# Two transformer layers on one core: another order for attention's product trees, a first q projection in four passes, wq rows ahead of the x tiles, other places for later loads

## The chip, the cores and the metric

The kernel runs on one core of a Trainium2 chip. The metric is the device time of one execution in microseconds (us). Each version was run several times; medians are quoted. A profile is one of the executions, recorded by the hardware profiler; its span is about 1.8 us shorter than the time of the same run (1616.3 against 1618.12 us).

Names: PE is TensorE (matmuls), PEld its weight loads, DVE VectorE, ACT ScalarE, SP the engine whose queue issues nearly all DMAs ("SPq" in the profile).

## The reference

```python
x = x + A(layernorm(x))      # attention, four times in all: A, B, A, B
x = x + B(layernorm(x))      # gated MLP
# A: qkv = x @ wqkv;  32 heads of 32;  each token attends to 8 tokens: itself and
#    those 2, 4, ... 14 back (dilation 2);  softmax;  @ wo
# B: (silu(x @ w1) * (x @ w3)) @ w2
```

x is 2048 tokens x 1024, F is 3584, everything in bf16.

## The kernel before

PE does the projections and the MLP. Attention itself has no matmuls: because each token sees only 8 others, DVE forms the products elementwise and adds them up in *trees*. Tokens are handled in chunks of 512 (c = 0 to 3), attention in halves of a chunk (256 tokens). In this program the order of the instructions on each engine is the order in which it emits them. A small clock model in the program (`now`, `pe()`, `dve()`) decides where DVE's attention steps are interleaved; it fixes an order, it does not wait for anything.

One tree multiplies and adds up 8 times; a product lives in one of two buffers (`scr`):

```python
scr = ctx.enter_context(tc.tile_pool(name="scr", bufs=2))
...
def tree(n, mul, dst):
    bufs = {}
    def first(i):                      # product, 128 x 2048
        bufs[i] = mul(i)
    def half(i, m):                    # add the upper half to the lower one
        b = bufs[i]
        if m > 1:
            nc.vector.tensor_tensor(b[:, 0:m, :], b[:, 0:m, :], b[:, m:2 * m, :], op=ALU.add)
        else:
            nc.vector.tensor_tensor(dst(i), b[:, 0, :], b[:, 1, :], op=ALU.add)
    yield 1.14, 0.0, lambda: first(0)
    for i in range(n):
        yield 0.605, 0.0, lambda: half(i, 4)
        if i:
            yield 0.21, 0.0, lambda: half(i - 1, 1)
        if i + 1 < n:
            yield 1.14, 0.0, lambda: first(i + 1)
        yield 0.34, 0.0, lambda: half(i, 2)
    yield 0.27, 0.0, lambda: half(n - 1, 1)
```

Each attention half runs two trees: one gives the scores, the other the output `oT`. PE then multiplies `oT` by wo in *output-projection tiles* of 128 tokens (16 matmuls named `po`). The first four of these (called tiles 1 to 4 below; 1 and 2 need the first half's oT, 3 and 4 the second's, that is the fourth tree) are placed among the projections of chunk 3.

At the start, wq (8 rows of 256 KB) and four token tiles of x come in while PE warms up; the first q projection is made tile by tile:

```python
load_tile(0, 0, 512, nc.sync); load_tile(0, 512, D, nc.scalar); load_tile(1, 0, D, nc.sync)
loads(0, 2)                    # wq rows 0, 1
load_tile(2, 0, D, nc.sync)
loads(2, 4)
load_tile(3, 0, D, nc.sync)
loads(4, 8)                    # ... then K's weights and x of chunk 1 (1 MB each)
...
warm(NWARM)                    # 13 matmuls on zeros
# (cut) tokens 0-127: kk outermost, as the wq rows arrive; tokens 128-255: block by block
tok = slice(2 * P, CH)         # tokens 256-511 in one pass
for i, acc in enumerate(accumulators(2, 2 * P)):
    for b in range(2):
        for kk in range(KT):
            product(acc[:, b, :], kk, 2 * i + b, tok, kk == 0, kk == KT - 1)
    nc.scalar.copy(hT[:, 2 * i:2 * i + 2, tok], acc[:])
    nc.sync.dma_start(q_rows[:, 2 * i:2 * i + 2, 0:CH], hT[:, 2 * i:2 * i + 2, :])
    then[i]()    # load_x(2), V's weights, V's weights, load_x(3)
```

Then comes K of chunk 0 (matmuls named `ps`), whose results go to DRAM by way of SP, four stores of two blocks each. The statistics of *all* chunks of x stand ahead of the first tree on DVE.

Of the kernel before, what the change touches and what calls it, by code (L numbers as in the profile page):

```python
# [15 lines left out]
def kernel(  # L16
# [13 lines left out]
    nc = tc.nc  # L30
# [17 lines left out]
    scale = float(Dh) ** -0.5  # L48
    EPS = 1e-5
    BOOST = 3000  # L50
    NWARM = 13
    fsplits = [(0, 16), (16, NF)] if NF > 16 else [(0, NF)]
    HTN = max(b - a for a, b in fsplits)

# [25 lines left out]


    MM, TABLE, DMA = 0.216, 1.3, 2.5
    now = dict(pe=22.0, dve=15.0, act=22.0, table=None)
    units = [(l, c) for l in range(2) for c in range(NCH)]
    norms, attention = [], []
    x_at = [12.5, 20.0, 25.0, 34.0]
    xnT_at, norm_left, qkv_at, oT_at, o_todo = {}, {}, {}, {}, {}

    def pe(n, ready=0.0):
# [137 lines left out]
        for part in parts:  # L227
            norms.append([part(key, c, r), None])

    def first_q(ws, loads, then):  # L230


        xnT = xnTs["Q", 0, 0] = xtp.tile([P, KT, CH], BF16, name="xnT")
        st = small.tile([P, TPC, 2, 6], FP32, name="st1", bufs=1)
        mv = small.tile([P, TPC, 2], FP32, name="mv1", bufs=1)
        sd = small.tile([P, TPC], FP32, name="sd1", bufs=1)
        rstd = small.tile([P, TPC], FP32, name="rstd1", bufs=1)
        q_rows = qkv_d[0][0][:].rearrange("i t s -> (i t) s").rearrange("(b p) s -> p b s", p=P)

        def load_tile(j, h0, h1, queue):  # L240
            queue.dma_start(x_sb[:, j, h0:h1], xin[:, j, h0:h1])  # L241

        load_tile(0, 0, 512, nc.sync)
        load_tile(0, 512, D, nc.scalar)
        load_tile(1, 0, D, nc.sync)
        loads(0, 2)
        load_tile(2, 0, D, nc.sync)
        loads(2, 4)
        load_tile(3, 0, D, nc.sync)
        loads(4, 8)  # L250
        preload = small.tile([P, 1], FP32, name="preload", bufs=1)
        nc.scalar.activation(preload[:], epst[:], ACTF.Sqrt)

        def stats(j, hh):
            nc.vector.bn_stats(st[:, j, hh, :], x_sb[:, j, hh * 512:(hh + 1) * 512])  # L255

        def deviation(j):
            nc.vector.bn_aggr(mv[:, j, :], st[:, j, :, :])
            nc.scalar.activation(sd[:, j:j + 1], mv[:, j, 1:2], ACTF.Sqrt, bias=epst[:])  # L259

        def apply(j, parts=1):
            nc.vector.reciprocal(rstd[:, j:j + 1], sd[:, j:j + 1])
            xn = xnp.tile([P, D], BF16, name="xn")
            for i in range(parts):
                d = slice(i * D // parts, (i + 1) * D // parts)
                nc.vector.tensor_scalar(xn[:, d], x_sb[:, j, d], mv[:, j, 0:1], rstd[:, j:j + 1],  # L266
                                        op0=ALU.subtract, op1=ALU.mult)
            return xn

        def transpose(xn):  # L270
            pTs = []
            for h in range(2):
                pT = psum.tile([P, KH, P], BF16, name="pT", tag="mm")
                for kk in range(KH):
                    nc.tensor.transpose(pT[:, kk, :], xn[:, (h * KH + kk) * P:(h * KH + kk + 1) * P], ident[:])  # L275
                pTs.append(pT)
            return pTs

        def evacuate(j, h, pTs, copy):
            copy(xnT[:, h * KH:(h + 1) * KH, j * P:(j + 1) * P], pTs[h][:])  # L280

        def product(out, kk, b, tok, start, stop):
            nc.tensor.matmul(out, lhsT=ws[kk // KH][:, kk % KH, b * P:(b + 1) * P], rhs=xnT[:, kk, tok],  # L283
                             start=start, stop=stop, skip_group_check=True)

        def accumulators(per, n):
            return [psum.tile([P, per, n], FP32, name="pq", tag="mm") for _ in range(KT // per)]

        warm(NWARM)
        stats(0, 0)  # L290
        stats(0, 1)
        deviation(0)
        stats(1, 0)
        xn = apply(0, 2)
        pTs = transpose(xn)
        evacuate(0, 0, pTs, nc.scalar.copy)
        stats(1, 1)
        evacuate(0, 1, pTs, nc.vector.tensor_copy)
        deviation(1)

        accs = accumulators(4, P)
        tok = slice(0, P)

        def step0(kk):
            for b in range(KT):
                product(accs[b // 4][:, b % 4, :], kk, b, tok, kk == 0 and b % 4 == 0, kk == KT - 1)

        for kk in range(6):
            step0(kk)
        stats(2, 0)  # L310
        xn = apply(1)
        pTs = transpose(xn)
        for h in range(2):
            evacuate(1, h, pTs, nc.scalar.copy)
        for kk in range(6, KT):
            step0(kk)
        stats(2, 1)
        deviation(2)
        for i in range(2):
            nc.scalar.copy(hT[:, 4 * i:4 * i + 4, tok], accs[i][:])  # L320

        accs = accumulators(4, P)
        tok = slice(P, 2 * P)

        def block1(b):
            for kk in range(KT):
                product(accs[b // 4][:, b % 4, :], kk, b, tok, kk == 0, kk == KT - 1)
            if b % 4 == 3:
                nc.scalar.copy(hT[:, b - 3:b + 1, tok], accs[b // 4][:])

        stats(3, 0)
        xn = apply(2)
        stats(3, 1)
        deviation(3)
        for b in range(3):
            block1(b)
        pTs = transpose(xn)
        for h in range(2):
            evacuate(2, h, pTs, nc.scalar.copy)
        xn = apply(3)  # L340
        for b in range(3, 5):
            block1(b)
        pTs = transpose(xn)
        evacuate(3, 0, pTs, nc.scalar.copy)
        evacuate(3, 1, pTs, nc.vector.tensor_copy)
        for b in range(5, KT):
            block1(b)

        tok = slice(2 * P, CH)
        for i, acc in enumerate(accumulators(2, 2 * P)):  # L350
            for b in range(2):
                for kk in range(KT):
                    product(acc[:, b, :], kk, 2 * i + b, tok, kk == 0, kk == KT - 1)
            nc.scalar.copy(hT[:, 2 * i:2 * i + 2, tok], acc[:])
            nc.sync.dma_start(q_rows[:, 2 * i:2 * i + 2, 0:CH], hT[:, 2 * i:2 * i + 2, :])
            then[i]()
        qkv_at[0, 0, 0] = now["act"] + DMA / 2

    def tree(n, mul, dst):

        bufs = {}

        def first(i):
            bufs[i] = mul(i)

        def half(i, m):
# [3 lines that stand above are left out]
            else:  # L370
                nc.vector.tensor_tensor(dst(i), b[:, 0, :], b[:, 1, :], op=ALU.add)  # L371

        yield 1.14, 0.0, lambda: first(0)
        for i in range(n):
            yield 0.605, 0.0, lambda: half(i, 4)
            if i:
                yield 0.21, 0.0, lambda: half(i - 1, 1)
            if i + 1 < n:
                yield 1.14, 0.0, lambda: first(i + 1)
            yield 0.34, 0.0, lambda: half(i, 2)  # L380
        yield 0.27, 0.0, lambda: half(n - 1, 1)

    qks, vs = {}, {}

# [296 lines left out]
    def load_wq(k0, k1):  # L681
        for kk in range(k0, k1):
            nc.sync.dma_start(w_tiles[kk // KH][:, kk % KH, :], wqkv_v[:, kk, 0:D])  # L683
        if k1 == KT:
            load_weight()
            load_weight()
            load_x(1)

    first_q(w_tiles[0:2], load_wq, (lambda: load_x(2), load_weight, load_weight, lambda: load_x(3)))
    xnT_at["Q", 0, 0], norm_left["Q", 0, 0] = now["pe"], 0  # L690
    queue_norm(("Q", 0, 1), 1, 0)
    queue_norm(("Q", 0, 1), 1, 1)
# [3 lines left out]
    for c in range(NCH):  # L696
        for which in range(3):
            if c == NCH - 1 and which == 0:
                o_queue += [(0, n) for n in range(TPC)]
            if c == NCH - 1 and which == 2:  # L700
                between(False, True)
            then = ()
            if c == 0 and which == 0:
                continue
            if c == 2 and which == 0:
                then = (None, None, lambda: nc.sync.dma_start(wo[:], wo_v))
            if c == 2 and which == 1:
                then = (load_weight, None, load_weight)
            q_part(0, c, which, w_tiles[2 * which:2 * which + 2], then)
            if c == NCH - 1:  # L710
                release(2)
            if which == 0 and 1 <= c < NCH - 1:
                for r in range(R):
                    queue_norm(("Q", 0, c + 1), c + 1, r, (norm_apply,))
# [44 lines left out]
```

## Time and profile before

| | before |
|---|---|
| median time (6 runs) | 1619.05 us (1618.66 to 1619.55) |
| span of the profiled run | 1616.3 us (the time of this run was 1618.12 us) |
| PE busy | 1610.7 us |
| DVE busy | 1176.6 us (73%) |
| first `ps` matmul | 24.64 us |
| first tree begins | 47.74 us |

The first lines of the page: span, and busy us, share of the span and instructions of each engine.

```profile
span 1616.3 us, 19263 instructions
...
PE 1610.7 (100%) x7609; PEld 805.3 (50%) x7609; DVE 1176.6 (73%) x1965; ACT 353.6 (22%) x547; POOL 1.9 (0%) x12
```

The chain of waits in order of time (start, us, what): followed back from the last instruction, it stays on PE from 16.48 us. The last line here is output-projection tile 3, in 3.45 us without a break. (The chain's times lie 0.16 to 0.17 us behind those of the timeline, below.)

```profile
16.48 8.33 PE pq L283 x88
24.80 113.96 PE ps L591 x528
...
159.49 3.45 PE po L552 x16
```

A 512-wide `ps` matmul takes 113.96 / 528 = 0.216 us. The Trainium skill, "TensorE: Matmul & The Clock Gate", section "Wait — 56ns, not 53.3ns?", gives N / 2.4 GHz plus about 2.5 ns for warm matmuls, 215.7 ns at N = 512; this trace agrees. So PE already runs there at the rate that the page calls warm, and what is left to gain is its waiting.

The timeline of the first 80 us (start us, duration us, engine, line, operation; in brackets the idle time before it and what ended it): the waits for wq rows, the first `ps`, the issue of x of chunk 3, the statistics of chunk 3, and the first trees.

```profile
8.92 0.45 PEld L283 LDWEIGHTS <-wqkv 128*128 128x128 bf16 x8 [0.24 <-DMA wqkv<-in_A_wqkv_dram]
...
10.24 0.45 PEld L283 LDWEIGHTS <-wqkv 128*128 128x128 bf16 x8 [0.87 <-DMA wqkv<-in_A_wqkv_dram]
...
24.64 55.63 PE L591 MATMUL ps<-xnT,wqkv 128*128 128x512 bf16 x257
...
25.86 0.98 SPq L677 DMA_DIRECT2D x_sb<-in_A_x_dram  x1
...
40.93 1.27 DVE L189 BATCH_NORM_STATS2 st<-x_sb 128x6 f32<-128x512 bf16 x2
...
47.74 1.21 DVE L424 TENSOR_TENSOR pr<-qT,kT 128x2048 bf16<-128x2048 bf16 x1
...
51.66 0.29 DVE L371 TENSOR_TENSOR psm<-pr 128x256 bf16<-128x256 bf16 x1
...
51.99 1.23 DVE L424 TENSOR_TENSOR pr<-qT,kT 128x2048 bf16<-128x2048 bf16 x1
...
54.38 1.23 DVE L424 TENSOR_TENSOR pr<-qT,kT 128x2048 bf16<-128x2048 bf16 x1
```

One step of a tree, product to product, takes 54.38 - 51.99 = 2.39 us; the product starts 0.33 us after the last small fold. x of chunk 3 (`x_sb`, L677) is issued at 25.86 us; its statistics run at 40.93 without a wait for a DMA.

Last, the wait of PE's weight loads for attention (us in total, times, longest), the one thing on PE that DVE delayed after the start:

```profile
PEld L552 <- DVE oT L371: 0.2, 1, 0.2
```

### The profile page before, as it was taken

The page shows a single profiled execution, that of the slowest core. Times are in us where ns is not written, and L with a number is a line of the kernel's source. Part 1 is how long each engine was busy: PE and PEld are TensorE (multiplying, and loading weights), DVE is VectorE, ACT ScalarE, POOL GpSimd, SP SyncE. Part 2 cuts the span into 40 slices and gives each one's busy share as a digit, 9 for nine tenths or more (in the row PEclk, how much of TensorE's full clock was granted, in tenths as well). Part 3 has the DMA queues.
Part 4 walks back from the last instruction along what each step waited for, and adds up shares of the span by engine and source line. Part 5 has one row for each costly group of instructions (what it writes and reads, how often), then busy time and mean ns, then how long its engine had stood idle before and what let it go on. Part 6 is the DMA issues. An engine that isn't in the chain of part 4 may idle for free.

```text
span 1616.3 us, 19263 instructions
## 1 busy us (share of the span) xinstructions
PE 1610.7 (100%) x7609; PEld 805.3 (50%) x7609; DVE 1176.6 (73%) x1965; ACT 353.6 (22%) x547; POOL 1.9 (0%) x12
## 2 busy tenths in 40 slices
PE   9999999999999999999999999999999999999999
PEld 6666544444445544455444554445544444444444
DVE  5999898989899899998998449983599832222212
ACT  4433311212112230222302123021230212011110
POOL 0000000000000000000000000000000000000000
PEclk9999999999999999999999999999999999999999
DMA  9565855466537773577553776528684266436440
GB/s 314 149 190 158 254 178 169 129 193 190 170 105 236 222 203 125 169 208 249 160 186 120 211 239 175 186 97 259 210 223 158 93 194 170 143 108 218 157 130 27
DMA packets 336427, 285.82 MB, mean 177 GB/s; under 512 B 69712, under 2 KB 318928, under 8 KB 336208
## 3 DMA queue, kind: packets, MB, share of 16 engines
q1 hardware_dynamic: 336192, 284.46, 58.0%
q8 instruction: 59, 0.97, 0.2%
q14 instruction: 32, 0.26, 0.0%
q10 hardware_dynamic: 144, 0.13, 0.0%
HBM read 239.47 MB, written 29.36 MB: 166 GB/s over the span
## 4 chain that ended last, share of the span: by engine, by line
PE 99%; DMA 0%; SPq 0%; DVE 0%; ACT 0%; issue 0%
PE acc L658 24%; PE pu L642 24%; PE pg L634 24%; PE ps L591 20%; PE po L552 7%; PE pq L283 1%; DMA wqkv<-in_A_wqkv_dram 0%; SPq L683 0%; SPq L241 0%; DVE xn L266 0%; ACT xnT L280 0%; PE pT L275 0%; DVE st L255 0%; ACT sd L259 0%; DVE x_sb L668 0%
## 5 line engine op out<-in xcount | busy, mean ns | idle before, releaser
L642 PE MATMUL pu<-xnT,w3t 128*128 128x512 bf16 x1792 | 423.4, 379 | 0.0
L634 PE MATMUL pg<-xnT,w1t 128*128 128x512 bf16 x1792 | 423.4, 379 | 0.0
L658 PE MATMUL acc<-w2t,hT 128*128 128x512 bf16 (+1 forms) x1804 | 389.7, 378 | 0.0
L591 PE MATMUL ps<-xnT,wqkv 128*128 128x512 bf16 x1472 | 319.2, 379 | 0.0
L638 ACT ACTIVATE sg<-pg 128x512 bf16<-128x512 f32 x224 | 133.6, 597 | 773.0 <-PE pg L634 719.4
L646 DVE TENSOR_TENSOR hT<-sg,pu 128x512 bf16<-128x512 bf16 x224 | 152.6, 681 | 186.8 <-PE pu L642 177.8
L658 PEld LDWEIGHTS <-hT 128*128 128x128 bf16 x1804 | 176.5, 98 | 210.5
L642 PEld LDWEIGHTS <-w3t 128*128 128x128 bf16 x1792 | 175.4, 98 | 211.4
L634 PEld LDWEIGHTS <-w1t 128*128 128x128 bf16 x1792 | 175.3, 98 | 211.4
L591 PEld LDWEIGHTS <-wqkv 128*128 128x128 bf16 x1472 | 211.1, 143 | 106.7
L424 DVE TENSOR_TENSOR pr<-qT,kT 128x2048 bf16<-128x2048 bf16 x128 | 156.2, 1221 | 87.2 <-DMA kT<-qkv_d 85.1
L668 DVE TENSOR_TENSOR x_sb<-x_sb,acc 128x512 bf16<-128x512 bf16 x129 | 87.3, 677 | 107.6 <-PE acc L658 107.4
L484 DVE TENSOR_TENSOR tm<-At,vT 128x2048 bf16<-128x2048 bf16 x128 | 156.1, 1220 | 2.4
L595 ACT CAST sgt<-ps 128x512 bf16<-128x512 f32 x184 | 106.7, 585 | 230.7 <-PE ps L591 211.9
L369 DVE TENSOR_TENSOR tm<-tm 128x1024 bf16<-128x1024 bf16 (+1 forms) x256 | 134.5, 550 | 0.4
L369 DVE TENSOR_TENSOR pr<-pr 128x1024 bf16<-128x1024 bf16 (+1 forms) x256 | 134.0, 551 | 0.5
L552 PE MATMUL po<-wo,oT 128*128 128x512 bf16 x512 | 115.7, 379 | 0.0
L552 PEld LDWEIGHTS <-oT 128*128 128x128 bf16 x512 | 50.1, 98 | 60.1 <-DVE oT L371 0.2
L189 DVE BATCH_NORM_STATS2 st<-x_sb 128x6 f32<-128x512 bf16 x120 | 75.9, 671 | 4.6 <-DMA x_sb<-in_A_x_dram 4.6
L557 DVE TENSOR_TENSOR x_sb<-x_sb,po 128x512 bf16<-128x512 bf16 x64 | 43.3, 684 | 19.2 <-PE po L552 18.9
L638 ACT ACT_TABLE_LOAD x31 | 39.8, 1283 | 51.2 <-PE pg L634 51.0
L446 DVE STREAM_TRANSPOSE psmT<-psm 128x2048 bf16<-128x2048 bf16 x16 | 36.9, 2306 | 0.2
(85 smaller groups left out, 402.3 us busy)
## 6 DMA issues: line engine op xcount, KB each, us to landing
w1t<-in_B_w_dram SPq DMA_DIRECT2D x56, 1024.0 KB, 5.5
w3t<-in_B_w_dram SPq DMA_DIRECT2D x56, 1024.0 KB, 8.0
w2t<-in_B_w_dram SPq DMA_DIRECT2D x48, 1024.0 KB, 5.4
wqkv<-in_A_wqkv_dram SPq DMA_DIRECT2D x28, 1024.0 KB, 6.8
qkv_d<-sgt SPq DMA_DIRECT2D x92, 256.0 KB, 2.9
qT<-qkv_d SPq DMA_DIRECT2D x16, 512.0 KB, 8.4
w2t<-in_B_w_dram SPq DMA_DIRECT2D x16, 512.0 KB, 5.2
kT<-qkv_d SPq DMA_DIRECT2D x14, 544.0 KB, 9.5
```

What stands on the lines that cost most here:

```text
L369: nc.vector.tensor_tensor(b[:, 0:m, :], b[:, 0:m, :], b[:, m:2 * m, :], op=ALU.add)
L424: V.tensor_tensor(pr[:], qT[:], kT[:, :, k0:k0 + TCH], op=ALU.mult)
L484: V.tensor_tensor(tm[:], At[:], win, op=ALU.mult)
L552: nc.tensor.matmul(ps[:], lhsT=oT[:, t, j * P:(j + 1) * P], rhs=wo[:, t, hh * 512:(hh + 1) * 512], start=(t == 0), stop=(t == KT - 1))
L591: nc.tensor.matmul(ps[:], lhsT=ws[kk // KH][:, kk % KH, t::KT], rhs=xnT[:, kk, :], start=(kk == 0), stop=(kk == KT - 1))
L595: nc.scalar.copy(sgt[:, t - t0, :], ps[:])
L634: nc.tensor.matmul(pg[:], lhsT=w1t[:, kk, fi * P:(fi + 1) * P], rhs=xnT[:, kk, :], start=(kk == 0), stop=(kk == KT - 1))
L638: nc.scalar.activation(sg[:], pg[:], ACTF.Silu)
L642: nc.tensor.matmul(pu[:], lhsT=w3t[:, kk, fi * P:(fi + 1) * P], rhs=xnT[:, kk, :], start=(kk == 0), stop=(kk == KT - 1))
L646: nc.vector.tensor_tensor(hT[:, f - f0, :], sg[:], pu[:], op=ALU.mult)
L658: nc.tensor.matmul(acc[:], lhsT=hT[:, f - f0, j * P:(j + 1) * P], rhs=w2ts[(f - f0) // 8][:, (f - f0) % 8, q0:q0 + step], start=(f == f0), ...
L668: nc.vector.tensor_tensor(xs, xs, acc[:], op=ALU.add)
```

## The change

Its intent is threefold: no DVE step of a tree should need the one directly ahead of it; wq rows should land earlier, so that the first pass does not wait for them; and each token tile gets its own pass, so that none waits for the next tile. Four things ride along: 12 warm-up matmuls instead of 13, a first evacuation in smaller pieces, q stored in two DMAs instead of four, and other places for the loads of x and of V's weights.

```diff
-    NWARM = 13
+    NWARM = 12
-    x_at = [12.5, 20.0, 25.0, 34.0]
+    x_at = [12.5, 21.0, 24.0, 36.0]          # clock model only
...
-        loads(0, 2)
+        loads(0, 4)
         load_tile(2, 0, D, nc.sync)
-        loads(2, 4)
+        loads(4, 8)
         load_tile(3, 0, D, nc.sync)
-        loads(4, 8)
+        load_weight(); load_weight()         # K
+        load_x(1)
+        load_x(2)
... (tile 0's evacuation in parts of 2, 2 and 4 blocks)
-        (one pass each for tiles 0 and 1, one of 256 tokens for tiles 2 and 3)
+        for j in range(1, TPC):              # one pass of 128 tokens each
... (in tree)
+        yield product(0)
+        yield fold(0, 4)
+        for i in range(0, n, 2):
+            yield product(i + 1)
+            yield fold(i, 2)
+            yield fold(i + 1, 4)
+            yield fold(i, 1)
+            yield fold(i + 1, 2)
+            if i + 2 < n:
+                yield product(i + 2)
+            yield fold(i + 1, 1)
+            if i + 2 < n:
+                yield fold(i + 2, 4)
... (projections of chunk 0)
-    first_q(..., (lambda: load_x(2), load_weight, load_weight, lambda: load_x(3)))
+            if c == 0 and which == 1:        # K: after its first and third store
+                then = (lambda: (load_weight(), load_weight()), None, lambda: load_x(3))
```

(`product(i)` is `first(i)` of before, `fold(i, m)` is `half(i, m)`.)

More of the change, by code (lines that the diff above doesn't have):

```diff
@@ L82 @@
     MM, TABLE, DMA = 0.216, 1.3, 2.5
-    now = dict(pe=22.0, dve=15.0, act=22.0, table=None)
+    now = dict(pe=23.6, dve=15.0, act=24.5, table=None)
     units = [(l, c) for l in range(2) for c in range(NCH)]
     norms, attention = [], []
-    x_at = [12.5, 20.0, 25.0, 34.0]
+    x_at = [12.5, 21.0, 24.0, 36.0]
     xnT_at, norm_left, qkv_at, oT_at, o_todo = {}, {}, {}, {}, {}
@@ L228, in queue_norm, with first_q @@
             norms.append([part(key, c, r), None])
-    def first_q(ws, loads, then):
+    def first_q(ws, loads):
         xnT = xnTs["Q", 0, 0] = xtp.tile([P, KT, CH], BF16, name="xnT")
@@ L245, in first_q @@
         load_tile(1, 0, D, nc.sync)
-        loads(0, 2)
+        loads(0, 4)
         load_tile(2, 0, D, nc.sync)
-        loads(2, 4)
+        loads(4, 8)
         load_tile(3, 0, D, nc.sync)
-        loads(4, 8)
+        load_weight()
+        load_weight()
+        load_x(1)
+        load_x(2)
         preload = small.tile([P, 1], FP32, name="preload", bufs=1)
@@ L268, in apply, with transpose, evacuate, product @@
             return xn
-        def transpose(xn):
+        def transpose(xn, cuts):
             pTs = []
-            for h in range(2):
-                pT = psum.tile([P, KH, P], BF16, name="pT", tag="mm")
-                for kk in range(KH):
-                    nc.tensor.transpose(pT[:, kk, :], xn[:, (h * KH + kk) * P:(h * KH + kk + 1) * P], ident[:])
-                pTs.append(pT)
-            return pTs
-        def evacuate(j, h, pTs, copy):
-            copy(xnT[:, h * KH:(h + 1) * KH, j * P:(j + 1) * P], pTs[h][:])
-        def product(out, kk, b, tok, start, stop):
-            nc.tensor.matmul(out, lhsT=ws[kk // KH][:, kk % KH, b * P:(b + 1) * P], rhs=xnT[:, kk, tok],
-                             start=start, stop=stop, skip_group_check=True)
-        def accumulators(per, n):
-            return [psum.tile([P, per, n], FP32, name="pq", tag="mm") for _ in range(KT // per)]
+            for k0, k1 in zip(cuts, cuts[1:]):
+                pT = psum.tile([P, k1 - k0, P], BF16, name="pT", tag="mm")
+                for kk in range(k0, k1):
+                    nc.tensor.transpose(pT[:, kk - k0, :], xn[:, kk * P:(kk + 1) * P], ident[:])
+                pTs.append((k0, k1, pT))
+            return pTs
+        def evacuate(j, part, copy):
+            k0, k1, pT = part
+            copy(xnT[:, k0:k1, j * P:(j + 1) * P], pT[:])
+        def product(j, out, kk, b, start):
+            nc.tensor.matmul(out, lhsT=ws[kk // KH][:, kk % KH, b * P:(b + 1) * P],
+                             rhs=xnT[:, kk, j * P:(j + 1) * P], start=start, stop=kk == KT - 1,
+                             skip_group_check=True)
+        def accumulators():
+            return [psum.tile([P, 4, P], FP32, name="pq", tag="mm") for _ in range(2)]
+        def keep(j, i, acc):
+            nc.scalar.copy(hT[:, 4 * i:4 * i + 4, j * P:(j + 1) * P], acc[:])
         warm(NWARM)
@@ L294, in first_q @@
         xn = apply(0, 2)
-        pTs = transpose(xn)
-        evacuate(0, 0, pTs, nc.scalar.copy)
+        p0, p1, p2 = transpose(xn, (0, 2, 4, 8))
+        evacuate(0, p0, nc.scalar.copy)
+        evacuate(0, p1, nc.scalar.copy)
         stats(1, 1)
-        evacuate(0, 1, pTs, nc.vector.tensor_copy)
+        evacuate(0, p2, nc.vector.tensor_copy)
         deviation(1)
-        accs = accumulators(4, P)
-        tok = slice(0, P)
-        def step0(kk):
-            for b in range(KT):
-                product(accs[b // 4][:, b % 4, :], kk, b, tok, kk == 0 and b % 4 == 0, kk == KT - 1)
@@ L308, in first_q @@
-        for kk in range(6):
-            step0(kk)
-        stats(2, 0)
-        xn = apply(1)
-        pTs = transpose(xn)
-        for h in range(2):
-            evacuate(1, h, pTs, nc.scalar.copy)
-        for kk in range(6, KT):
-            step0(kk)
+        xn = apply(1)
+        stats(2, 0)
         stats(2, 1)
         deviation(2)
-        for i in range(2):
-            nc.scalar.copy(hT[:, 4 * i:4 * i + 4, tok], accs[i][:])
-        accs = accumulators(4, P)
-        tok = slice(P, 2 * P)
@@ L325, in block1 @@
-        def block1(b):
-            for kk in range(KT):
-                product(accs[b // 4][:, b % 4, :], kk, b, tok, kk == 0, kk == KT - 1)
-            if b % 4 == 3:
-                nc.scalar.copy(hT[:, b - 3:b + 1, tok], accs[b // 4][:])
-        stats(3, 0)
-        xn = apply(2)
-        stats(3, 1)
-        deviation(3)
-        for b in range(3):
-            block1(b)
-        pTs = transpose(xn)
-        for h in range(2):
-            evacuate(2, h, pTs, nc.scalar.copy)
-        xn = apply(3)
@@ L341, in first_q @@
-        for b in range(3, 5):
-            block1(b)
-        pTs = transpose(xn)
-        evacuate(3, 0, pTs, nc.scalar.copy)
-        evacuate(3, 1, pTs, nc.vector.tensor_copy)
-        for b in range(5, KT):
-            block1(b)
-        tok = slice(2 * P, CH)
-        for i, acc in enumerate(accumulators(2, 2 * P)):
-            for b in range(2):
-                for kk in range(KT):
-                    product(acc[:, b, :], kk, 2 * i + b, tok, kk == 0, kk == KT - 1)
-            nc.scalar.copy(hT[:, 2 * i:2 * i + 2, tok], acc[:])
-            nc.sync.dma_start(q_rows[:, 2 * i:2 * i + 2, 0:CH], hT[:, 2 * i:2 * i + 2, :])
-            then[i]()
+        accs = accumulators()
@@ new lines, in first_q @@
+        for kk in range(KT):
+            for b in range(KT):
+                product(0, accs[b // 4][:, b % 4, :], kk, b, kk == 0 and b % 4 == 0)
+            if kk == 4:
+                parts = transpose(xn, (0, 4, 8))
+                for part in parts:
+                    evacuate(1, part, nc.scalar.copy)
+        for i in range(2):
+            keep(0, i, accs[i])
+        for j in range(1, TPC):
+            if j + 1 < TPC:
+                xn = apply(j + 1)
+            if j + 2 < TPC:
+                for hh in range(2):
+                    stats(j + 2, hh)
+                deviation(j + 2)
+            for i, acc in enumerate(accumulators()):
+                for b in range(4):
+                    for kk in range(KT):
+                        product(j, acc[:, b, :], kk, 4 * i + b, kk == 0)
+                    if j + 1 < TPC and (i, b) == (1, 0):
+                        parts = transpose(xn, (0, 4, 8))
+                        for part in parts:
+                            evacuate(j + 1, part, nc.scalar.copy)
+                keep(j, i, acc)
+                if j == TPC - 1:
+                    nc.sync.dma_start(q_rows[:, 4 * i:4 * i + 4, 0:CH], hT[:, 4 * i:4 * i + 4, :])
@@ L371, in half, with product, fold @@
                 nc.vector.tensor_tensor(dst(i), b[:, 0, :], b[:, 1, :], op=ALU.add)
-        yield 1.14, 0.0, lambda: first(0)
-        for i in range(n):
-            yield 0.605, 0.0, lambda: half(i, 4)
-            if i:
-                yield 0.21, 0.0, lambda: half(i - 1, 1)
-            if i + 1 < n:
-                yield 1.14, 0.0, lambda: first(i + 1)
-            yield 0.34, 0.0, lambda: half(i, 2)
-        yield 0.27, 0.0, lambda: half(n - 1, 1)
+        def product(i):
+            return 1.14, 0.0, lambda: first(i)
+        def fold(i, m):
+            return {4: 0.605, 2: 0.34, 1: 0.205}[m], 0.0, lambda: half(i, m)
+        yield product(0)
[11 more added lines that the diff above has]
+                yield fold(i + 2, 4)
     qks, vs = {}, {}
@@ L683, in load_wq @@
             nc.sync.dma_start(w_tiles[kk // KH][:, kk % KH, :], wqkv_v[:, kk, 0:D])
-        if k1 == KT:
-            load_weight()
-            load_weight()
-            load_x(1)
-    first_q(w_tiles[0:2], load_wq, (lambda: load_x(2), load_weight, load_weight, lambda: load_x(3)))
+    first_q(w_tiles[0:2], load_wq)
     xnT_at["Q", 0, 0], norm_left["Q", 0, 0] = now["pe"], 0
```

## The prediction

> **What bounds it.** TensorE. The page gives PE 1610.7 of 1616.3 us busy. The chain of waits, in order of time, shows one unbroken run of PE work from 16.48 to 1613.38 us; a 512-wide matmul repeats every 0.216 us (528 in 113.96 us). That is the full warm rate in the Trainium skill, "TensorE: Matmul & The Clock Gate", section on 56 ns against 53.3 ns (N / 2.4 GHz plus about 2.5 ns); PEclk is 1.00 throughout. PE's waits sum to 2.6 us, all before 11 us. VectorE is busy 73% but off the chain: the only PE instruction that waited for attention's oT is one weight load, 0.2 us. So only the start, up to the first ps matmul at about 24.7 us (timeline), and the untouched tail of 3 us can set the time.
>
> **Product trees.** Before, the next product follows at once on the last fold of the product two back, whose buffer it overwrites: start to start 0.33 us (51.66 to 51.99), against 0.20 us where an unrelated instruction follows (144.70 to 144.90). After, another fold stands between. About 0.12 us x 6 joints x 32 trees = 23 us of VectorE (step of 2.40 us becomes about 2.28). Worth 0 on the span.
>
> **First q projection.** Removed: waits for wq rows. Before, x tiles 2 and 3 go between the rows; weight loads wait 0.24, 0.87 and 0.23 us for rows 3, 4, 5, which land at about 8.9, 10.2, 10.9 us, one 256 KB slot each 0.66 us. After, rows 4 to 7 move up one slot: about 9.55, 10.2, 10.9, 11.55 us. The first pass ends at about 12.05 us instead of 12.8; tile 1's transposes (0.45 us) sit between rows. First products start some 0.3 us earlier (smaller first evacuation), but row 4 then governs. NWARM 12: the last warm matmul still ends near 5.9 us, xn comes at 6.3; nothing, while the clock stays warm.
> Added: the last 256 tokens go as two passes of 128: 64 x 0.109 = 6.98 us become 128 x 0.057 = 7.3 us, +0.35 us. The 0.29 us wait for xn of tile 3 disappears.
> Sum: 12.05 + 192 x 0.057 + 2 x 0.45 = 23.9 us to the first ps matmul, against 24.7: about -0.8 us.
>
> **Moved.** V's weights are issued only after the first K store, about 28.5 to 29.5 us (before 22.4 and 24.4), and must land by about 37.7 and 38.6 us. 2 MB at the 400 GB/s seen in the windows is 5.2 us, plus latency: about 34 and 36.5 us. In before, one DMA transpose held the queue for 6.05 us (26.94) behind 3 MB of backlog; after, the backlog is small. If held so long again, PE waits 1 to 3 us at the first V matmuls. x of chunk 3 lands at about 40 us, when its statistics ran before (40.9): neutral.
>
> **Prediction.** 1618.2 us, range 1617.0 to 1619.8 (8 in 10), a gain of 0.05%. Faster by over 2%: 0.005; within 2%: 0.985; slower: 0.01.
>
> **What would show it.** First ps matmul at 23.9 us (23.4 to 24.4); PE waits for wqkv at most 0.6 us a row; first ps to end unchanged at 1591.6 us. About 2.28 us per product step; VectorE busy 10 to 25 us lower; ps, pg, pu, acc unchanged in count and mean (379 ns). The oT wait goes, as the third output-projection tile moves one group later.
> Wrong if: a PE gap near 38 us at ps (V weights late); matmuls at half rate near 6 to 7 us (warm-up too short); first ps later than 24.7 us (passes or evacuations stall); the step stays at 2.40 us (the wait was not the buffer's reuse); any new PE wait for oT or hT after 40 us.

## The result, and the profile after

| | before | after |
|---|---|---|
| median time (6 runs each) | 1619.05 us | 1619.41 us (1618.72 to 1619.91) |
| ratio of fast runs | | 1.0002, 95% interval 0.9989 to 1.0015 |
| span of the profiled run | 1616.3 us | 1616.9 us (time 1618.72 us) |
| DVE busy | 1176.6 us | 1166.3 us |
| first `ps` matmul | 24.64 us | 23.59 us |
| first tree begins | 47.74 us | 54.58 us |
| tile 3 of the output projection, to the next `ps` | 3.46 us | 5.11 us |

A ratio is the mean time of one kernel's fast runs over that of the other's of the same rounds, so it is not quite the ratio of the medians. The total hardly moved. The profile shows two effects that nearly cancel. The page, and in it the chain's shares by line (shown for after because DVE lines now stand in it):

```profile
span 1616.9 us, 19388 instructions
...
PE 1610.4 (100%) x7672; PEld 805.8 (50%) x7672; DVE 1166.3 (72%) x1964; ACT 353.2 (22%) x549; POOL 1.9 (0%) x12
...
PE acc L655 24%; PE pu L639 24%; PE pg L631 24%; PE ps L588 12%; PE po L549 6%; DVE pr L421 1%; DVE tm L481 1%; DVE tm L355 1%; DVE pr L355 1%; PE pq L287 1%; DMA wqkv<-in_A_wqkv_dram 1%; DVE st L189 1%; DMA x_sb<-in_A_x_dram 0%; DVE At L465 0%; DVE L L445 0%; DVE xn L214 0%
```

The timeline of the first 80 us, in answer to that of before:

```profile
9.48 0.45 PEld L287 LDWEIGHTS <-wqkv 128*128 128x128 bf16 x8 [0.62 <-DMA wqkv<-in_A_wqkv_dram]
...
23.59 56.72 PE L588 MATMUL ps<-xnT,wqkv 128*128 128x512 bf16 x262
...
34.16 0.59 ACT L592 CAST sgt<-ps 128x512 bf16<-128x512 f32 x1 [0.86 <-PE ps L588]
...
34.92 5.44 SPq L217 DMA_TRANSPOSE xnT<-xn  x2
...
40.46 0.53 SPq L597 DMA_DIRECT2D qkv_d<-sgt  x1
...
41.05 0.47 SPq L674 DMA_DIRECT2D x_sb<-in_A_x_dram  x1
...
47.75 1.28 DVE L189 BATCH_NORM_STATS2 st<-x_sb 128x6 f32<-128x512 bf16 x2 [8.88 <-DMA x_sb<-in_A_x_dram]
...
54.58 1.20 DVE L421 TENSOR_TENSOR pr<-qT,kT 128x2048 bf16<-128x2048 bf16 x1
```

PE reaches K 1.05 us earlier (23.59 against 24.64). But x of chunk 3 is issued at 41.05 us instead of 25.86: it stands behind K's third store, whose data ACT finished at 34.16 + 0.59 = 34.75 us but which SP could issue only at 40.46, after two DMA transposes that occupied the queue for 5.44 us. x landed at 47.7 us, DVE stood still for 8.88 us, and the first tree began 6.84 us later than before.

The timeline of PE around the third output-projection tile of after (before: the unbroken 3.45 us of tile 3 in the chain above):

```profile
161.73 1.46 PE L549 MATMUL po<-wo,oT 128*128 128x512 bf16 x6
164.23 0.39 PE L549 MATMUL po<-wo,oT 128*128 128x512 bf16 x1 [1.04 <-DVE oT L357]
164.89 2.12 PE L549 MATMUL po<-wo,oT 128*128 128x512 bf16 x9 [0.27 <-DVE oT L357]
166.84 3.62 PE L588 MATMUL ps<-xnT,wqkv 128*128 128x512 bf16 x16
```

The tile takes 166.84 - 161.73 = 5.11 us instead of 3.46: 1.65 us lost (the idle times add up to only 1.31, because the duration of a recorded matmul, 0.38 us, is longer than its 0.216 us share of PE, and two such overhangs lie in the gaps). -1.05 + 1.65 = +0.60 us is the whole difference of the two spans. (Tile 3 begins later in after than in before although PE is ahead: it stands one group of 16 `ps` matmuls later, which gave attention 3.45 us more. Without that the loss would have been larger: an estimate from 6.84 us of lateness against 3.45 us of room.)

Two steps of a tree of after, from DVE's timeline:

```profile
59.04 1.22 DVE L421 TENSOR_TENSOR pr<-qT,kT 128x2048 bf16<-128x2048 bf16 x1
...
60.98 1.22 DVE L421 TENSOR_TENSOR pr<-qT,kT 128x2048 bf16<-128x2048 bf16 x1
...
63.58 1.22 DVE L421 TENSOR_TENSOR pr<-qT,kT 128x2048 bf16<-128x2048 bf16 x1
```

Two steps take 63.58 - 59.04 = 4.54 us, so one takes 2.27 instead of 2.39 to 2.40.

### The profile page after: what moved, and what is told of

It reads as the page before. It is cut to its first block, busy times and chain, and to the rows that moved or that the text cites. A ratio compares the mean times of both kernels' runs of the same rounds, so it can differ in the third digit from the quotient of the medians.

```text
span 1616.9 us, 19388 instructions
## 1 busy us (share of the span) xinstructions
PE 1610.4 (100%) x7672; PEld 805.8 (50%) x7672; DVE 1166.3 (72%) x1964; ACT 353.2 (22%) x549; POOL 1.9 (0%) x12
## 4 chain that ended last, share of the span: by engine, by line
PE 91%; DVE 7%; DMA 1%; SPq 0%; issue 0%; ACT 0%; ACTq 0%; DVEq 0%
PE acc L655 24%; PE pu L639 24%; PE pg L631 24%; PE ps L588 12%; PE po L549 6%; DVE pr L421 1%; DVE tm L481 1%; DVE tm L355 1%; DVE pr L355 1%; PE pq L287 1%; DMA wqkv<-in_A_wqkv_dram 1%; DVE st L189 1%; DMA x_sb<-in_A_x_dram 0%; DVE At L465 0%; DVE L L445 0%; DVE xn L214 0%
## 5 line engine op out<-in xcount | busy, mean ns | idle before, releaser
L465 DVE STREAM_TRANSPOSE At<-AeT 128x2048 bf16<-128x2048 bf16 x16 | 36.9, 2305 | 0.1
```

## The experiments

My theory: the start gained 1.05 us; the late load of chunk 3's x cost 1.65 us; the faster trees limited that loss. The rivals: the trees are worth nothing; or the new start, and not the load, delays attention. Eleven runs were made, in three calls (each call on one chip); three of them repeat a kernel unchanged. All were correct.

### x3_early: one DMA put back in time

```diff
-  then = (lambda: (load_weight(), load_weight()), None, lambda: load_x(3))
+  then = (lambda: (load_weight(), load_weight(), load_x(3)),)
```

> The changed kernel with one DMA moved: x of chunk 3 is issued right behind V's weights instead of after K's third store; no instruction of TensorE, VectorE or ScalarE changes its place. Theory (the change gained 1.05 us at the start and lost 1.65 us because chunk 3's x landed at 47.7 us, so that attention began 6.8 us late and the third output-projection tile waited for oT): x lands by about 39 us, VectorE's 8.9 us wait goes, the first product tree starts at 45.5 to 48 us (54.6 in the changed kernel), PE's waits for oT are 0, first ps still at 23.6 us, last matmul at about 1612.3 us; time about 1.65 us below the changed kernel and 1.0 to 1.3 us below before, so 1617.7 us. Rival (the new tree order or the longer run of four passes costs the time): PE still waits 1 us or more for oT, time 1619.4 us.

Measured: 1617.39 us median, 5 runs (1616.77 to 1617.57); before 1619.03; ratio 0.9988, interval 0.9976 to 1.0001. The timeline of its profile:

```profile
29.90 0.51 SPq L674 DMA_DIRECT2D x_sb<-in_A_x_dram  x1
...
41.32 1.29 DVE L189 BATCH_NORM_STATS2 st<-x_sb 128x6 f32<-128x512 bf16 x2 [1.96 <-DMA x_sb<-in_A_x_dram]
...
48.46 1.21 DVE L421 TENSOR_TENSOR pr<-qT,kT 128x2048 bf16<-128x2048 bf16 x1
```

No PE wait for oT is left; tile 3 takes 3.45 us (162.24 to 165.69). x landed 2 us later than expected, and the first `ps` came at 24.10, not 23.6 us, because in this run wq row 4 landed late (0.9 us wait). The main point holds: this one load, without any change in the order of PE, DVE or ACT, takes 2.0 us off the changed kernel's median (measured in another call; 2.5 us in the same call, below).

### after_old_trees: the trees' share

```diff
-  (the new order of product and fold)
+  (the order of before)
```

> The changed kernel with the tree order of before; TensorE's order is unchanged. Theory (the new order shortens a product step from 2.40 to 2.27 us and so makes up part of the late start; the third output-projection tile needs the fourth tree): 4 trees x 6 joints x 0.13 = 3.1 us more delay, so PE waits for oT 4 to 5 us in all, time about 1622.4 us. Rival (the tree order is worth nothing to the span, as the prediction had it): 1619.4 us, PE's wait for oT unchanged at 1.3 us.

Measured: 1624.31 us median (1623.31 to 1625.46), ratio 1.0033, interval 1.0019 to 1.0046. The direction is that of the theory, the size is larger: tile 3 took 172.00 - 161.81 = 10.19 us. PE's timeline, and then the windows of 2 us (for each: busy us and instructions of PE, PEld, DVE, ACT, POOL, the granted clock of PE, the DMA share and GB/s):

```profile
161.81 1.31 PE L538 MATMUL po<-wo,oT 128*128 128x512 bf16 x5
165.13 0.39 PE L538 MATMUL po<-wo,oT 128*128 128x512 bf16 x1 [2.01 <-DVE oT L357]
167.52 2.55 PE L538 MATMUL po<-wo,oT 128*128 128x512 bf16 x5 [2.01 <-DVE oT L357]
...
172.00 4.08 PE L577 MATMUL ps<-xnT,wqkv 128*128 128x512 bf16 x16
```

```profile
164.00:166.00 2.00, 0.39 (x1) 0.10 (x1) 1.97 (x4) 0.00 (x0) 0.00 (x0) 1.00 1.05 251
166.00:168.00 2.00, 0.48 (x1) 0.10 (x1) 1.97 (x6) 0.00 (x0) 0.00 (x0) 0.53 0.92 226
168.00:170.00 2.00, 1.94 (x5) 0.72 (x6) 1.97 (x4) 0.00 (x0) 0.00 (x0) 0.50 1.07 352
```

So the wait was followed by a second harm: PE's clock fell to half. From 168.59 to 172.86 us ten weight loads are 0.43 us apart instead of 0.216; that is about 10 x 0.21 = 2.1 us, the part that the expectation lacked (10.19 - 5.11 = 5.1 us in all, where 3.1 had been worked out). The rival falls: once attention is late, each step of the trees counts.

### before_x3_late: the move alone, in the kernel before

```diff
-  first_q(..., (lambda: load_x(2), load_weight, load_weight, lambda: load_x(3)))
+  first_q(..., (lambda: load_x(2), load_weight, load_weight, lambda: None))
+  if c == 0 and which == 1:
+      then = (None, None, lambda: load_x(3))
```

> The kernel before with one DMA moved the other way: x of chunk 3 is issued after K's third store, as the change does; nothing else moves. Theory (this move alone is what delays attention): VectorE waits 6 to 9 us for x, the first tree starts at about 54 us instead of 47.7, and with the slow tree order PE waits 5 to 6.5 us for oT near 160 us; first ps stays at 24.6 us; time 1624 to 1625.5 us. Rival (the wait for oT comes from the rearranged start or the later V weights, not from this load): 1619 us, no PE wait for oT.

Measured: 1627.15 us (1626.26 to 1628.12), ratio 1.0049, interval 1.0037 to 1.0062. x was issued at 42.41 us, DVE waited 9.13 us for it, the first tree began at 55.55 us, PE waited 6.4 us for oT, and the clock fell to half again (0.50 in the windows from 164 to 172 us), which the expectation had not counted. The first `ps` came at 24.94 us (24.64 in before). So the move of this load is enough, without the new start or the later weights.

### before_new_trees: the trees alone, in the kernel before

```diff
-  (the old order in tree)
+  (the new order of product and fold)
```

> The kernel before with the new tree order alone; TensorE's order is unchanged. Theory (VectorE is off the chain of waits while x comes in time): a product step takes 2.27 us instead of 2.40, VectorE's busy time falls by about 10 us, the one 0.2 us weight-load wait for oT goes, the time stays at 1619.0 us within 0.4. Rival (VectorE's speed sets the span somewhere): 1 us or more faster.

Measured: 1618.01 us (1617.95 to 1618.73); before 1619.03 (9 runs, 1618.89 to 1619.71); ratio 0.9994, interval 0.9982 to 1.0007. DVE was busy for 1167.8 us. The expectation failed by about half a us: the median is 1.0 us lower, and no run of the one overlaps one of the other in this call, though the interval includes 1. That calls for an explanation, because the profile of before had shown no loss of that size.

### before_again: was the profile of before typical?

The profiled run of before took 1618.12 us, less than any of its six timed runs. It was therefore profiled once more, unchanged.

> The kernel before, unchanged, profiled a second time. Its profiled run was its fastest (1618.12 us; the timed ones had a median of 1619.05), and in it the eighth weight load of the third output-projection tile waited only 0.2 us for oT. Theory (before sits on the edge: oT and TensorE arrive there together, and a normal run has PE wait for oT): the first tree starts 0.3 to 1.2 us later than 47.74 us and PE waits 0.3 to 1.2 us for oT. That would also explain why the new trees alone gained 1.0 us. Rival (before has no such wait in a normal run): PE's wait for oT at most 0.2 us though the run takes 1619 us.

Measured: 1619.1 us, span 1617.3 (1.0 us more than the first profile). PE's timeline of this run:

```profile
159.37 1.46 PE L552 MATMUL po<-wo,oT 128*128 128x512 bf16 x6
161.11 0.39 PE L552 MATMUL po<-wo,oT 128*128 128x512 bf16 x1 [0.28 <-DVE oT L371]
161.77 2.12 PE L552 MATMUL po<-wo,oT 128*128 128x512 bf16 x9 [0.27 <-DVE oT L371]
163.72 3.62 PE L591 MATMUL ps<-xnT,wqkv 128*128 128x512 bf16 x16
```

and, from the timelines of ACT and DVE in the same run, what came just before its first tree:

```profile
47.85 0.58 ACT L595 CAST sgt<-ps 128x512 bf16<-128x512 f32 x1 [3.17 <-DMA qkv_d<-sgt]
...
48.66 0.17 DVE L201 RECIPROCAL rstd<-sd 128x2 f32<-128x2 f32 x1 [1.43 <-ACT sd L194]
```

The first tree began at 48.75 us, 1.0 us later than in the first profile, and tile 3 took 4.35 us, 0.9 us more than its 3.45. So this run of the *kernel before* lost 0.9 us at the same place, and the profile that the prediction rested on was a lucky one. The first `ps` was at 24.69 us, so the start was not the cause. The two lines show what was: ACT's cast waited 3.17 us (1.73 in the first profile) for an earlier store of its staging buffer; the standard deviation that stands behind it on ACT came late; and DVE, whose first tree stands behind the reciprocal, waited 1.43 us for it instead of 0.42. In the profile of the new trees alone the same wait was 1.10 us and the first tree began at 48.50 us, almost as late, yet PE had no wait for oT. So the lost 0.9 us is the likely source of the 1.0 us of the new trees; with two profiles of the one and one of the other it is not shown for every run.

### before_three_scr: what the 0.13 us of a step is

In the compiled instruction list of before, the third and every later product of a tree carries a wait on DVE's own semaphore, that is, on the instruction just ahead, the last reader of the buffer that it overwrites; with a third buffer this wait is gone and the order of all instructions is the same:

```
two buffers:    TensorTensor psm<-pr 128x256 [waits DVE]   TensorTensor pr<-qT,kT 128x2048 [waits DVE]
three buffers:  TensorTensor psm<-pr 128x256 [waits DVE]   TensorTensor pr<-qT,kT 128x2048
```

```diff
-  scr = ctx.enter_context(tc.tile_pool(name="scr", bufs=2))
-  xnp = ctx.enter_context(tc.tile_pool(name="xn", bufs=4))
+  scr = ctx.enter_context(tc.tile_pool(name="scr", bufs=3))
+  xnp = ctx.enter_context(tc.tile_pool(name="xn", bufs=2))      # pays for the memory
```

> The kernel before, old tree order, with three buffers instead of two for the products (paid for with two buffers instead of four for the normalised x); no instruction changes its place. Theory (0.13 us a step is the wait of the next product for the last reader of the buffer that it overwrites): a step falls from 2.40 to 2.27 us without any reordering, VectorE's busy time by about 10 us, and the time as with the new trees alone, 1618.0 to 1618.6 us. Rival (the pause comes from two successive instructions of these shapes, whatever the buffers): step stays 2.40 us, time 1619 us.

Measured, DVE's timeline:

```profile
58.32 0.28 DVE L371 TENSOR_TENSOR psm<-pr 128x256 bf16<-128x256 bf16 x1
58.53 1.22 DVE L424 TENSOR_TENSOR pr<-qT,kT 128x2048 bf16<-128x2048 bf16 x1
...
60.60 0.28 DVE L371 TENSOR_TENSOR psm<-pr 128x256 bf16<-128x256 bf16 x1
60.80 1.22 DVE L424 TENSOR_TENSOR pr<-qT,kT 128x2048 bf16<-128x2048 bf16 x1
```

A step takes 60.80 - 58.53 = 2.27 us and the product starts 0.2 us after the small fold, in the *old* order. So the gain of a step comes from removing the wait for the reuse of the buffer, and not from the order as such. The time was a miss: 1630.37 us (ratio 1.0075). Halving the buffers of the normalised x made DVE wait 17.5 us in all for DMA transposes to release them (6.9 us of it at 39.5 us, ahead of the first tree, which began at 54.40), so PE waited 7.1 us for oT. The kernel tells about the step, and says nothing about the time of a third buffer.

### x3_early_three_passes: is a pass of 128 dearer?

```diff
+  (x of chunk 3 early)
-  for j in range(1, TPC): ... one pass of 128 tokens per tile
+  pass of tile 1, with the transposes of tiles 2 and 3 in it; then one pass of 256 tokens
```

> The changed kernel with x of chunk 3 early and the last two token tiles of the first q projection in one pass of 256 again. Theory (two passes of 128 cost 0.35 us more than one of 256, and tile 3's transposes fit into the second pass): first ps 0.35 us earlier than with four passes, 23.2 to 23.8 us, PE's waits for oT still 0, time 1616.9 to 1617.2 us. Rival (tile 3 comes too late for a pass of 256, which is why the change splits it): a wait of TensorE for xn or xnT of 0.3 us or more, first ps not earlier.

Measured: 1617.15 us (1616.72 to 1617.24), ratio 0.9990, interval 0.9978 to 1.0003; the first `ps` at 23.68 us. The expected 0.35 us did not come: from the transposes of tile 2 to the first `ps` it is 23.68 - 14.29 = 9.39 us here and 23.59 - 14.21 = 9.38 us in the changed kernel. The passes of 128 cost 0.056 us a matmul (88 in 4.91 us), not the 0.057 that was used; 128 x 0.0558 = 7.14 against 64 x 0.109 = 6.98 us would leave 0.16. The trace shows where that went: the first matmul of the 256-token pass starts at 16.70 us, 0.22 us after the last one of tile 1's pass (16.47) instead of 0.056, and the copy of tile 3's transposes that it reads (DVE, 16.28, 0.42 us long) ends at 16.70. So the rival has a small part: tile 3 comes about 0.17 us too late for a pass of 256. The `--waits` view lists no wait there, because a recorded matmul is longer than its share of PE and covers the gap.

### x3_early_rows_mixed: the rows' share of the start

```diff
+  (x of chunk 3 early)
-  loads(0, 4); load_tile(2); loads(4, 8); load_tile(3)
+  loads(0, 2); load_tile(2); loads(2, 4); load_tile(3); loads(4, 8)
```

> The changed kernel with x of chunk 3 early and the x tiles 2 and 3 between the wq rows again, as before. Theory (rows 4 to 7 land one 0.66 us slot later): the first pass ends about 0.6 us later and first ps is at 24.3 to 24.7 us; time 0.5 to 0.7 us above the version with the rows ahead, about 1617.9 us. Rival (the four passes and the smaller first evacuation give the gain of the start, not the rows): first ps at 23.6 to 24.1 us as with the rows ahead.

Measured: 1617.83 us (1617.72 to 1618.22), ratio 0.9996, interval 0.9982 to 1.0009; the first `ps` at 24.39 us. Row 4 is used at 10.18 us, where the three-pass kernel (rows ahead) uses it at 9.56, and 0.71 us separate the two at the first `ps`, and 0.68 us the medians. The size rests on this pair, since row 4's use varies from run to run: it is at 9.17 to 10.01 us in the seven profiles with the rows ahead (first `ps` 23.31 to 24.10) and at 10.12 to 11.41 us in the six with the rows mixed (24.39 to 25.93). The two groups do not overlap; most of the 1.05 us that the start gained is the order of the rows.

### after_again, x3_early_again, x3_early_warm13: the comparison on one chip

The changed kernel and the corrected one again, and the corrected one with `NWARM = 13`.

> The changed kernel, unchanged, on the same chip as the corrected version. Its profiled run was its fastest (1618.72 us; median 1619.41). Theory: in a normal run the first tree starts at 54.5 to 55.5 us and PE waits 1.3 to 2.3 us for oT; time 0 to 0.6 us above before. Rival (the wait was a feature of that one run): no wait, time 1617.5 us.

> The changed kernel with x of chunk 3 issued behind V's weights, a second time, on the same chip as the changed kernel. Theory: PE's wait for oT 0 again; 1.3 to 2.0 us below before and 1.6 to 2.3 us below the changed kernel. Rival (the first result owed something to its chip): less than 0.8 us below before.

> The same with 13 warm-up matmuls instead of 12. Theory (the twelfth ends 0.5 us before xn, so the thirteenth fills a wait): the first transposes start at 6.3 us either way, first ps within 0.2 us of the version with 12 in the same call, time the same within 0.3 us. Rival (12 leave the clock at half rate at the start): with 13 the first transposes and products run faster and the time falls by 0.3 us or more.

| | median (5 runs) | range | ratio to before | interval |
|---|---|---|---|---|
| before (9 runs) | 1618.93 us | 1618.02 to 1619.98 | | |
| changed kernel | 1619.85 us | 1619.54 to 1621.49 | 1.0007 | 0.9995 to 1.0020 |
| x of chunk 3 early | 1617.31 us | 1617.05 to 1617.52 | 0.9991 | 0.9977 to 1.0004 |
| the same, 13 warm-ups | 1617.18 us | 1616.75 to 1617.80 | 0.9990 | 0.9977 to 1.0002 |

The changed kernel was 0.9 us above before (0 to 0.6 had been expected) and 2.5 us above the corrected one (1.6 to 2.3). Its profile fell on its slowest run this time: the first tree at 55.61 us, tile 3 took 169.64 - 161.83 = 7.81 us. PE's idle times for oT are 2.05 and 0.27 us, and the clock fell:

```profile
161.83 1.46 PE L549 MATMUL po<-wo,oT 128*128 128x512 bf16 x6
165.34 0.39 PE L549 MATMUL po<-wo,oT 128*128 128x512 bf16 x1 [2.05 <-DVE oT L357]
166.00 3.80 PE L549 MATMUL po<-wo,oT 128*128 128x512 bf16 x9 [0.27 <-DVE oT L357]
169.64 3.62 PE L588 MATMUL ps<-xnT,wqkv 128*128 128x512 bf16 x16
```

```profile
166.00:168.00 2.00, 2.00 (x5) 0.73 (x6) 1.97 (x3) 0.00 (x0) 0.00 (x0) 0.52 1.04 355
168.00:170.00 2.00, 2.00 (x7) 0.91 (x6) 2.00 (x4) 0.00 (x0) 0.00 (x0) 0.63 1.09 370
```

The corrected kernel again has no wait for oT (first `ps` 23.62 us, tile 3 in 3.45 us); the rival about the chip falls. The 95% intervals of its ratio just include 1; but all ten of its runs (1616.77 to 1617.57) lie below all 18 runs of before (1618.02 to 1619.98). With 13 warm-ups the time is the same. Its first `ps` was 0.31 us earlier, which is outside the 0.2 us expected; but row 4 also came 0.36 us earlier in that run (used at 9.17 instead of 9.53), so this does not show a merit of the thirteenth.

## Why the prediction was right or wrong

The measured 1619.41 us lies inside the stated range (1617.0 to 1619.8), but that was luck: a gain of about the size forecast at the start was given back by a loss that the prediction had called neutral.

- **The start: right.** The prediction said -0.8 us and a first `ps` at 23.9 us (23.4 to 24.4). It was 23.59, and -1.05 us; row 4 came at 9.48 us where 9.55 was said. The rows carry most of it (0.71 us in the mixed-rows experiment).
- **The passes of 128: mis-sized.** The term +0.35 us measured 0.0 net (9.39 against 9.38 us): the two passes cost 0.16 us more, and the one pass of 256 that they replace would have begun 0.17 us late.
- **V's weights: right.** They were issued at 28.3 us; no PE gap near 38 us.
- **The step that failed: "x of chunk 3 lands at about 40 us, when its statistics ran before (40.9): neutral."** It landed at 47.7 us. The data of K's third store was ready at 34.75 us; but on SP's queue the DMAs went out in order, and the store and the load behind it stood behind DMA transposes. The prediction had seen one transpose hold the queue for 6.05 us, and had asked what that would do to V's weights; it did not ask the same for the load behind the third store. The Trainium skill, "DMA: Bandwidth & Descriptors", section "Anatomy of one DMA — SWDGE (gpsimd) path", says that a semaphore wait of a DMA happens on the issuing sequencer before it is dispatched. It says so where it describes the GpSimd path; what the trace shows on SP's queue is the order (5.7 us from data ready to issue, 5.44 of them the two transposes; x then took 6.67 us to land).
- **"Worth 0 on the span" for the trees: wrong.** The trees alone took 1.0 us off the median of before (interval 0.9982 to 1.0007), and without them the changed kernel took 1624.31 us. DVE's step was predicted well (2.28 us; it is 2.27) and so was its cause. What failed is the step from "the only PE instruction that waited for attention's oT is one weight load, 0.2 us" to "off the chain". The 0.2 us of wait meant that the slack at that tile was zero, and the profiled run was faster than all six timed runs; in the second profile the same place lost 0.9 us.
- **"The oT wait goes": wrong.** Moving tile 3 one group later gave 3.45 us, the late tree took 6.84; PE waited 1.31 us. (With x early the wait does go.)

What became of the expected gain, then: -1.05 us at the start, given back by 1.65 us at tile 3 in the profiled run. The version that keeps both gains (x of chunk 3 issued right behind V's weights) is about 1.6 us (0.1%) faster than before and 2.0 to 2.5 us faster than the changed kernel by the medians; its intervals against before just include 1. The corrected kernel with the old trees was not run, so how much of this gain the trees bring is open.

## What to carry to other kernels

A wait of 0.2 us in one profile can mean that there is no slack at all at that place: ask how early the data comes, not only how long the engine waited, and see whether the profiled run was a typical one. When a load is moved in a queue that issues in order, as SP's did here, look at what stands between its old and its new place: its issue time is set by everything ahead of it, here a store that was ready and two transposes that blocked it. An engine that is "off the chain" is off it only as long as its first input arrives on time.

## What the Trainium skill lacked or had wrong

- "TensorE: Matmul & The Clock Gate", sections "HAM oscillation — how this bites in real kernels" and "Why this matters for your kernels" (HAM is the page's name for what sets PE's clock): they warn of PE idle gaps above about 3.4 us (or 3 us). Here the clock fell to half after shorter gaps: 2.05 us, one matmul and 0.27 us in the repeated changed kernel (granted clock 0.52 in the next window), and 2.01 us, one matmul and part of a second gap of 2.01 us in the one with the old trees (0.53 from 166 to 168 us); it did not fall after 1.04 and 0.27 us. One matmul between two gaps did not prevent it. No run here looked for the length at which it falls.
- "VectorE: DVE Perf Modes", section "The DRAIN you can't avoid": in its test of eight copies a semaphore after each operation costs nothing extra. Here a product that waits for the small fold directly ahead (0.29 us long) starts 0.33 us after that fold's start, and without this wait (third buffer) 0.20 us after it: 0.13 us each time. In this kernel DVE was busy about 10 us less without these waits (1176.6 us before, 1167.4 with the third buffer, 1166.3 to 1167.8 with the new order).
- "DMA: Bandwidth & Descriptors" does not say how long one DMA transpose of this size occupies the queue that issues it, nor that the time varies, so that it can hold up everything behind it for several us: here 1.23 us at least, 1.29 median and 6.05 at most among the 60 of the kernel before. The longest came right behind 1 MB loads (6.05 us; in the changed kernel 1.40 us without such a load just before it, 3.26 right behind two); that these lengthen it was not tested.
